# First row tile by halves, norm chunks one pair later, a fourth matmul group further behind, and a last row in narrower column groups

## The chip, the cores and the metric

The kernel runs on one core of a Trainium2 chip. The metric is the device time of one execution in microseconds (us). A profiled execution also has a span, which is 1.7 to 1.9 us shorter than its device time.

## The reference

The reference is the output of a block and its vector-Jacobian product, ten arrays in all. Cut to what matters here:

```python
xn  = layernorm(q)                       # 2048 rows x 1024
out = q + A(xn, k, v, ...) + B(xn, W_gate, W_up, W_down)
# A: shift convolution, long convolution by FFT, times xn
# B: h = relu(xn @ W_gate) * (xn @ W_up);  h @ W_down        (1024 -> 3584 -> 1024)
outputs = out and d(out).grad_out for q, k, v, shift_k, ssm_k, ssm_D, W_gate, W_up, W_down
```

## The kernel before

TensorE is shared by two branches. The branch of B norms the rows, goes through seven blocks of 512 hidden columns (gate, up and gradient matmuls for each row tile of 128), then makes the weight gradients, the output and the gradient of the input. The branch of A does its Fourier transforms as matmuls in between. Four places are touched.

The norm works in chunks of row tiles, (1, 1, 1, 1, 2, 2, 2, 2, 2, 2). It is a generator; each chunk takes three steps:

```python
V.tensor_scalar(out=b(2), in0=b(1), scalar1=LN_EPS, scalar2=None, op0=ALU.add)
V.tensor_copy(out=f(3), in_=b(2))                                     # cast before the root
self.ln_act = nc.scalar.activation(out=f(4), in_=f(3), func=ACT.Sqrt)
yield
root = V.reciprocal(out=f(6), in_=f(4))
...
V.tensor_copy(out=f(10), in_=b(3))                                    # cast after it
self.ln_dve = V.reciprocal(out=self.rstd[:, st0:st0 + n], in_=f(10))
for j in range(n):
    V.tensor_scalar(out=xt[:, j, :], in0=xt[:, j, :], scalar1=self.rstd[:, st:st + 1], ...)   # whole row
    nc.gpsimd.dma_start(out=xn_d[...], in_=xt[:, j, :])               # normalised rows to HBM
```

`flip_xn` transposes a normalised row tile on TensorE and copies it out of PSUM. The first column block (`ahead`) takes the rows two tiles at a time; after each pair one more chunk of the norm is put in, which only matters for later:

```python
yield from grad(sp)
...
if ahead and sp + 4 < HS:
    yield from gate_up(sp + 4)
    chunk()
if n == 1 and sp < 4:
    chunk()
if ahead and sp == 4:
    ... tables()             # Sin tables for branch A
```

PSUM is the memory that the matmuls write their sums to; an eviction is the instruction that takes a finished group out of it and so frees its buffer. `four` makes four PSUM groups of the weight gradients at once. In its first half the fourth group goes one step behind the other three:

```python
for st in range(h + 1):
    for i in range(3 if st < h else 0):
        mm(i, st)
    if st > 0:
        mm(3, st - 1)
```

`grad_x`, the last stage, makes the input's gradient of a row tile in two column groups of 512, each with two reductions on VectorE, then two sums over both, then two last multiplies on ScalarE and two adds.

Branch A starts by loading the normalised rows that the norm has stored, into a tile named xt. The load is issued on the same queue (SyncE's) as all the weights:

```python
def load_xn(self, st):
    xt = st["xt"] = self.xp.tile([P, 16, P], BF16, name="xt")
    self.load_time(xt, self.xn_d, st["cg"])
```

## Time and profile before

| what | value |
|---|---|
| median time at the start (3 runs) | 1929.28 us, from 1925.44 to 1932.4 |
| span of the profiled execution | 1928.7 us |
| TensorE's largest wait, for an eviction near 45 us | 3.4 us |
| its waits for normalised rows, 9 to 30 us | 2.4 us in four |
| its wait in the fourth group of a weight gradient, at 893 us | 0.8 us |
| from its last matmul to the end of the span | 7.96 us |

TensorE is busy for 99% of the span, so only these gaps can be won. A timeline line reads: start, duration, engine, source line, operation, output and input tiles with shapes, how many instructions are merged, and in brackets the idle time before and what ended it. The prediction below shows the lines of the waits, of the start and of the tail.

VectorE's order while the row tiles 4 and 5 (counted from 0, here and below) are normed, and the transposes that wait for it:

```profile
23.54 0.17 DVE L764 CAST ln_s<-ln_b 128x2 f32<-128x2 bf16 x1
...
23.74 0.88 DVE L766 TENSOR_SCALAR ln_x<-ln_x,ln_s 128x1024 bf16<-128x1024 bf16 x2
...
24.54 0.68 DVE L906 SCALAR_TENSOR_TENSOR ru<-ru,ps_u 128x512 bf16<-128x512 bf16 x1
...
29.67 1.07 PE L835 MATMUL pst_x<-ident,ln_x 128*128 128x128 bf16 x16 [0.76 <-DVE ln_x L787]
```

The chunk's subtraction of the mean (L766) comes ahead of an eviction of PSUM (L906). The fourth group's wait, with the matmuls in it:

```profile
893.06 1.24 PE L1063 MATMUL ps_d<-g_nat,hs 128*128 128x512 bf16 x5 [0.84 <-ACT wo L1115]
```

### The profile page before, as it was taken

The page shows a single profiled execution, that of the slowest core. Times are in us where ns is not written, and L with a number is a line of the kernel's source. Part 1 is how long each engine was busy: PE and PEld are TensorE (multiplying, and loading weights), DVE is VectorE, ACT ScalarE, POOL GpSimd, SP SyncE. Part 2 cuts the span into 40 slices and gives each one's busy share as a digit, 9 for nine tenths or more (in the row PEclk, how much of TensorE's full clock was granted, in tenths as well). Part 3 has the DMA queues.
Part 4 walks back from the last instruction along what each step waited for, and adds up shares of the span by engine and source line. Part 5 has one row for each costly group of instructions (what it writes and reads, how often), then busy time and mean ns, then how long its engine had stood idle before and what let it go on. Part 6 is the DMA issues. An engine that isn't in the chain of part 4 may idle for free.

```text
span 1928.7 us, 36213 instructions
## 1 busy us (share of the span) xinstructions
PE 1909.5 (99%) x15526; PEld 881.6 (46%) x15526; DVE 910.5 (47%) x1378; ACT 633.8 (33%) x866; POOL 15.3 (1%) x38
## 2 busy tenths in 40 slices
PE   8999999999999999999999999999999999999998
PEld 3444444444444444444444444444444444444443
DVE  6767767767777754443534444400122222222222
ACT  5754354364354354354354344311000000000000
POOL 1000000000000000000000000000000000000000
PEclk9999999999999999999999999999999999999999
DMA  9975788974874982655662733384999854554451
GB/s 247 265 183 138 181 180 182 222 183 134 185 189 134 249 228 78 173 129 174 164 173 78 173 95 122 104 257 160 239 245 266 200 135 120 120 120 118 118 122 35
DMA packets 616017, 319.08 MB, mean 165 GB/s; under 512 B 450984, under 2 KB 585136, under 8 KB 615856
## 3 DMA queue, kind: packets, MB, share of 16 engines
q1 hardware_dynamic: 605360, 295.79, 62.9%
q10 hardware_dynamic: 9216, 16.78, 2.9%
q0 software_dynamic: 1280, 4.20, 0.6%
q8 instruction: 121, 1.98, 0.4%
q14 instruction: 40, 0.33, 0.1%
HBM read 141.56 MB, written 95.44 MB: 123 GB/s over the span
## 4 chain that ended last, share of the span: by engine, by line
PE 96%; issue 1%; DMA 1%; DVE 1%; ACT 1%; DVEq 0%; SPq 0%; ACTq 0%
PE ps_w L1050 20%; PE ps_x L1232 19%; PE ps_o L1198 10%; PE ps_h L806 10%; PE ps_u L806 10%; PE ps_g L806 10%; PE ps_d L1050 9%; PE ps L72 7%; PE ps_d L1063 1%; PE ps_w L1063 1%; ACT ln_j L743 0%; PE pst L308 0%; DMA ln_x<-in_A_q_dram 0%; DMA wu<-in_B_W_up_dram 0%; DMA wg<-in_B_W_gate_dram 0%
## 5 line engine op out<-in xcount | busy, mean ns | idle before, releaser
L1050 PE MATMUL ps_w<-ugs,xn_nat 128*128 128x512 bf16 x1728 | 383.7, 379 | 0.0
L806 PEld LDWEIGHTS <-xnT 128*128 128x128 bf16 x1792 | 170.5, 98 | 210.4 <-issue 10.6
L1050 PEld LDWEIGHTS <-xn_nat 128*128 128x128 bf16 x1728 | 165.0, 98 | 199.3 <-issue 5.5
L806 PE MATMUL ps_h<-wdT,goT 128*128 128x512 bf16 x896 | 207.7, 382 | 3.4 <-DVE ru L906 3.4
L806 PE MATMUL ps_u<-wu,xnT 128*128 128x512 bf16 x896 | 206.7, 379 | 1.7 <-DMA wu<-in_B_W_up_dram 1.7
L1251 ACT ACTIVATE w<-xn,m 128x512 f32<-128x512 bf16 x32 | 24.3, 807 | 559.0 <-issue 317.2
L806 PE MATMUL ps_g<-wg,xnT 128*128 128x512 bf16 x896 | 206.8, 379 | 1.1 <-DVE xnT L838 0.8
L1232 PE MATMUL ps_x<-wgT,ggT 128*128 128x512 bf16 x896 | 198.6, 379 | 0.0
L1232 PE MATMUL ps_x<-wuT,guT 128*128 128x512 bf16 x896 | 198.6, 379 | 0.0
L1198 PE MATMUL ps_o<-wd,hT 128*128 128x512 bf16 x896 | 193.6, 379 | 0.0
L1050 PE MATMUL ps_d<-g_nat,hs 128*128 128x512 bf16 x768 | 171.9, 379 | 0.0
L1232 PEld LDWEIGHTS <-ggT 128*128 128x128 bf16 x896 | 87.7, 98 | 105.7
L1198 PEld LDWEIGHTS <-hT 128*128 128x128 bf16 x896 | 87.7, 98 | 105.7
L1232 PEld LDWEIGHTS <-guT 128*128 128x128 bf16 x896 | 87.7, 98 | 105.7
L806 PEld LDWEIGHTS <-goT 128*128 128x128 bf16 x896 | 85.6, 98 | 107.0 <-issue 8.1
L319 DVE STREAM_TRANSPOSE flp<-C 128x1024 f32<-128x1024 f32 x48 | 90.5, 1931 | 83.3 <-ACT C L76 83.3
L906 DVE SCALAR_TENSOR_TENSOR ru<-ru,ps_u 128x512 bf16<-128x512 bf16 x112 | 76.5, 683 | 110.3 <-issue 48.6
L967 ACT CAST gh<-ps_h 128x512 bf16<-128x512 f32 x112 | 65.3, 584 | 162.0 <-PE ps_h L806 151.0
L1234 DVE CUSTOM_DVE_ANT_0 gx<-ps_x,gy 128x512 f32<-128x512 f32 x32 | 22.1, 691 | 198.1 <-PE ps_x L1232 198.1
L1148 ACT CAST wi<-ps_w 128x512 bf16<-128x512 f32 x108 | 63.7, 590 | 157.4 <-PE ps_w L1050 152.7
L76 ACT CAST C<-ps 128x1024 bf16<-128x1024 f32 x96 | 92.5, 1015 | 67.1 <-PE ps L72 66.1
L319 DVE STREAM_TRANSPOSE flp<-B 128x1024 f32<-128x1024 f32 x48 | 90.9, 1939 | 47.8 <-ACT B L76 47.8
(172 smaller groups left out, 1519.4 us busy)
## 6 DMA issues: line engine op xcount, KB each, us to landing
ug_d<-ru SPq DMA_DIRECT2D x112, 256.0 KB, 3.6
ugs<-ug_d SPq DMA_DIRECT2D x112, 256.0 KB, 5.2
wg<-in_B_W_gate_dram SPq DMA_DIRECT2D x56, 256.0 KB, 4.3
wu<-in_B_W_up_dram SPq DMA_DIRECT2D x56, 256.0 KB, 3.8
h_d<-ht SPq DMA_DIRECT2D x112, 128.0 KB, 2.1
hs<-h_d SPq DMA_DIRECT2D x56, 256.0 KB, 5.4
out_dram<-wi SPq DMA_DIRECT2D x56, 256.0 KB, 4.0
gt<-in_grad_out_dram SPq DMA_DIRECT2D x32, 256.0 KB, 3.9
```

Of the source, the lines that this page charges most:

```text
L72: self.pri.pin(self.nc.tensor.matmul(out, lhsT=lhsT, rhs=rhs, start=start, stop=stop))
L76: self.pri.pin(self.nc.scalar.copy(out=out, in_=in_))
L319: self.pri.pin(self.nc.vector.transpose(out=df[:, c0:c0 + 32, :], in_=sf[:, c0:c0 + 32, :]))
L806: self.pri.pin(self.nc.tensor.matmul(ps[:], lhsT=xT[:, kt * P:(kt + 1) * P], rhs=w(kt), start=(kt == 0), stop=(kt == self.DT - 1)), always ...
L906: self.pri.pin(nc.vector.scalar_tensor_tensor(out=ru[s][:, 1, :], in0=ru[s][:, 0, :], scalar=0.0, in1=ps[:], op0=ALU.is_gt, op1=ALU.mult))
L967: self.pri.pin(nc.scalar.copy(out=gh[:], in_=ps[:]))
L1050: self.pri.pin(self.nc.tensor.matmul(ps[:], lhsT=lhsT(st), rhs=rhs(st), start=(st == 0), stop=(st == self.ST - 1)))
L1063: self.pri.pin(self.nc.tensor.matmul(ps[i][:], lhsT=lhsT(i, st), rhs=rhs(i, st), start=(st == 0), stop=(st == self.ST - 1)))
L1148: self.pri.pin(nc.scalar.copy(out=wo[0][:, d, :], in_=ps[:]))
L1198: nc.tensor.matmul(ps[:], lhsT=hT[:, kt, :], rhs=self.wd[:, kt, oc], start=(kt == 0), stop=(kt == self.FT - 1))
L1232: nc.tensor.matmul(ps[:], lhsT=T[:, kt, :], rhs=W[:, kt, oc], start=(i == 0), stop=(i == n - 1))
L1251: nc.scalar.activation(out=w[:, oc], in_=xn[:, oc], func=ACT.Identity, scale=m[:, 5:6], bias=m[:, 4:5])
```

## The change

The intent has four parts: start the first matmul earlier by norming and transposing the first row tile in halves, and drop two casts of every chunk; move two norm chunks one pair of row tiles on, so that VectorE does not stand on a late load; let the fourth group lag by three steps, so that its PSUM buffer is free when it is needed; and cut the last row tile into column groups of 512, 256 and 256, so that less work follows the last matmul. The core of the diff:

```diff
-            V.tensor_copy(out=f(3), in_=b(2))
-            self.ln_act = nc.scalar.activation(out=f(4), in_=f(3), func=ACT.Sqrt)
+            self.ln_act = nc.scalar.activation(out=f(4), in_=b(2), func=ACT.Sqrt)
 ...
-            V.tensor_copy(out=f(10), in_=b(3))
-            self.ln_dve = V.reciprocal(out=self.rstd[:, st0:st0 + n], in_=f(10))
+            self.ln_dve = V.reciprocal(out=self.rstd[:, st0:st0 + n], in_=b(3))
 ...
+                for c in (0, 512) if st == 0 else (0,):
+                    xc = xt[:, j, c:c + (512 if st == 0 else D)]
+                    V.tensor_scalar(out=xc, in0=xc, scalar1=self.rstd[:, st:st + 1], ...)
 ...   # flip_xn: transposes and copy in two halves for st == 0
                 if ahead and sp + 4 < HS:
                     yield from gate_up(sp + 4)
+                if ahead and sp in (2, 4):
                     chunk()
 ...   # four
-        for st in range(h + 1):
+        lag = 3
+        for st in range(h + lag):
             for i in range(3 if st < h else 0):
                 mm(i, st)
-            if st > 0:
-                mm(3, st - 1)
+            if st >= lag:
+                mm(3, st - lag)
 ...   # grad_x
-            for ob in range(2):
-                oc = slice(ob * 512, ob * 512 + 512)
+            cuts = (0, 512, 768, D) if last else (0, 512, D)
+            for ob in range(len(cuts) - 1):
+                oc = slice(cuts[ob], cuts[ob + 1])
 ...   # sums added up group by group, the scaled add right behind each group
```

More of the change, by code (lines that the diff above doesn't have):

```diff
@@ L779, in layer_norm @@
                 self.tc.keep_in_program_order(root)
-            V.scalar_tensor_tensor(out=f(5), in0=f(3), scalar=0.5, in1=f(6), op0=ALU.mult, op1=ALU.mult)
+            V.scalar_tensor_tensor(out=f(5), in0=b(2), scalar=0.5, in1=f(6), op0=ALU.mult, op1=ALU.mult)
             V.scalar_tensor_tensor(out=b(3), in0=f(4), scalar=0.5, in1=f(5), op0=ALU.mult, op1=ALU.add)
-            V.tensor_copy(out=f(10), in_=b(3))
-            self.ln_dve = V.reciprocal(out=self.rstd[:, st0:st0 + n], in_=f(10))
+            self.ln_dve = V.reciprocal(out=self.rstd[:, st0:st0 + n], in_=b(3))
             self.pri.now()
@@ L786, in layer_norm @@
                 st = st0 + j
-                V.tensor_scalar(out=xt[:, j, :], in0=xt[:, j, :], scalar1=self.rstd[:, st:st + 1], scalar2=None,
-                                op0=ALU.mult)
+                for c in (0, 512) if st == 0 else (0,):
+                    xc = xt[:, j, c:c + (512 if st == 0 else D)]
+                    V.tensor_scalar(out=xc, in0=xc, scalar1=self.rstd[:, st:st + 1], scalar2=None, op0=ALU.mult)
                 nc.gpsimd.dma_start(out=xn_d[st * P:(st + 1) * P, :], in_=xt[:, j, :])
@@ L832, in flip_xn @@
     def flip_xn(self, st):
-        pst = self.ps.tile([P, self.DT, P], BF16, name="pst_x", tag="bps")
-        for kt in range(self.DT):
-            self.pri.pin(self.nc.tensor.transpose(pst[:, kt, :], self.xn[st][:, kt * P:(kt + 1) * P], self.ident[:]),
-                         always=True)
         xT = self.act_tile("xnT", st)
-        copied = self.nc.vector.tensor_copy(out=xT[:], in_=pst[:].rearrange("p a b -> p (a b)"))
-        if st < 4:
-            self.tc.keep_in_program_order(copied)
+        h = self.DT // 2 if st == 0 else self.DT
+        for k0 in range(0, self.DT, h):
+            pst = self.ps.tile([P, self.DT, P], BF16, name="pst_x", tag="bps")
+            for kt in range(k0, k0 + h):
+                self.pri.pin(self.nc.tensor.transpose(pst[:, kt, :], self.xn[st][:, kt * P:(kt + 1) * P],
+                                                      self.ident[:]), always=True)
+            copied = self.nc.vector.tensor_copy(out=xT[:, k0 * P:(k0 + h) * P],
+                                                in_=pst[:, k0:k0 + h, :].rearrange("p a b -> p (a b)"))
+            if st < 4:
+                self.tc.keep_in_program_order(copied)
         return xT
@@ L1064, in mm @@
                                                stop=(st == self.ST - 1)))
-        for st in range(h + 1):
+        lag = 3
+        done = 0
+        for st in range(h + lag):
             for i in range(3 if st < h else 0):
                 mm(i, st)
-            if st > 0:
-                mm(3, st - 1)
-            if st % 2 == 0 and st:
+            if st >= lag:
+                mm(3, st - lag)
+            if st % 2 and st > lag:
                 yield 1730
                 self.tick()
-                freed(st - 2)
-                freed(st - 1)
+                while done <= st - lag:
+                    freed(done)
+                    done += 1
+        while done < h:
+            freed(done)
+            done += 1
         for i in range(4):
@@ L1224, in grad_x @@
             w = p_ev.tile([P, D], F32, name="w")
-            m = p_sm.tile([P, 8], F32, name="m")
-            for ob in range(2):
-                oc = slice(ob * 512, ob * 512 + 512)
-                ps = self.ps_tile("ps_x")
+            m = p_sm.tile([P, 10], F32, name="m")
+            sums = m[:, 0:6].rearrange("p (a b) -> p a b", b=3)
+            hd = tc.keep_in_program_order
+            last = st == self.ST - 1
+            cuts = (0, 512, 768, D) if last else (0, 512, D)
+            for ob in range(len(cuts) - 1):
+                oc = slice(cuts[ob], cuts[ob + 1])
+                ps = self.ps_tile("ps_x")[:, 0:cuts[ob + 1] - cuts[ob]]
                 i, n = 0, 2 * self.FT
@@ L1231, in grad_x @@
                     for kt in range(self.FT):
-                        nc.tensor.matmul(ps[:], lhsT=T[:, kt, :], rhs=W[:, kt, oc], start=(i == 0), stop=(i == n - 1))
+                        nc.tensor.matmul(ps, lhsT=T[:, kt, :], rhs=W[:, kt, oc], start=(i == 0), stop=(i == n - 1))
                         i += 1
-                V.tensor_tensor_reduce(out=gx[:, oc], in0=ps[:], in1=gy[:, oc], scale=1.0, scalar=0.0, op0=ALU.add,
+                V.tensor_tensor_reduce(out=gx[:, oc], in0=ps, in1=gy[:, oc], scale=1.0, scalar=0.0, op0=ALU.add,
@@ L1235, in grad_x @@
                                        op1=ALU.add, accum_out=m[:, ob:ob + 1])
                 V.tensor_tensor_reduce(out=pr[:, oc], in0=gx[:, oc], in1=xn[:, oc], scale=1.0, scalar=0.0,
-                                       op0=ALU.mult, op1=ALU.add, accum_out=m[:, 2 + ob:3 + ob])
-                if ob == 0:
-                    self.tc.keep_in_program_order(V.scalar_tensor_tensor(
-                        out=gx[:, oc], in0=gx[:, oc], scalar=self.rstd[:, st:st + 1], in1=gt[:, oc], op0=ALU.mult,
-                        op1=ALU.add))
@@ L1242, in grad_x @@
-            hd = self.tc.keep_in_program_order
-            hd(V.tensor_tensor(out=m[:, 4:6], in0=m[:, 0:4].rearrange("p (a b) -> p a b", b=2)[:, :, 0],
-                               in1=m[:, 0:4].rearrange("p (a b) -> p a b", b=2)[:, :, 1], op=ALU.add))
-            hd(V.tensor_scalar(out=m[:, 6:8], in0=m[:, 4:6], scalar1=-1.0 / D, scalar2=None, op0=ALU.mult))
-            hd(V.tensor_scalar(out=m[:, 4:6], in0=m[:, 6:8], scalar1=self.rstd[:, st:st + 1], scalar2=None,
-                               op0=ALU.mult))
+                                       op0=ALU.mult, op1=ALU.add, accum_out=m[:, 3 + ob:4 + ob])
@@ new lines, in grad_x @@
+                if ob:
+                    hd(V.tensor_tensor(out=m[:, 6:8], in0=m[:, 6:8] if ob > 1 else sums[:, :, 0], in1=sums[:, :, ob],
+                                       op=ALU.add))
+                if ob + 2 == len(cuts):
+                    hd(V.tensor_scalar(out=m[:, 8:10], in0=m[:, 6:8], scalar1=-1.0 / D, scalar2=None, op0=ALU.mult))
+                    hd(V.tensor_scalar(out=m[:, 6:8], in0=m[:, 8:10], scalar1=self.rstd[:, st:st + 1], scalar2=None,
+                                       op0=ALU.mult))
@@ L1248, in grad_x @@
+                hd(V.scalar_tensor_tensor(out=gx[:, oc], in0=gx[:, oc], scalar=self.rstd[:, st:st + 1],
+                                          in1=gt[:, oc], op0=ALU.mult, op1=ALU.add))
             o1 = p_ev.tile([P, D], BF16, name="o1")
@@ L1250, in grad_x @@
                 oc = slice(ob * 512, ob * 512 + 512)
-                nc.scalar.activation(out=w[:, oc], in_=xn[:, oc], func=ACT.Identity, scale=m[:, 5:6], bias=m[:, 4:5])
-                if ob:
-                    hd(V.scalar_tensor_tensor(out=gx[:, oc], in0=gx[:, oc], scalar=self.rstd[:, st:st + 1],
-                                              in1=gt[:, oc], op0=ALU.mult, op1=ALU.add))
+                nc.scalar.activation(out=w[:, oc], in_=xn[:, oc], func=ACT.Identity, scale=m[:, 7:8], bias=m[:, 6:7])
                 V.tensor_tensor(out=o1[:, oc], in0=gx[:, oc], in1=w[:, oc], op=ALU.add)
```

## The prediction

> **What bounds the kernel now.** I read the page's busy shares first, then TensorE's own list of waits, then the timeline in order of time around the start, around each of TensorE's waits, and at the end, and last the issue and landing times of the transfers up to 125 us.
>
> The busy table of the page, with busy us, share and instruction count per engine:
>
> ```profile
> PE 1909.5 (99%) x15526; PEld 881.6 (46%) x15526; DVE 910.5 (47%) x1378; ACT 633.8 (33%) x866; POOL 15.3 (1%) x38
> ```
>
> TensorE is idle for only 1928.7 - 1909.5 = 19.2 us, so a change that leaves the matmuls alone can win at most about 1%. The list of TensorE's waits (total us, times, longest) says where that is:
>
> ```profile
> PE ps_h L806 <- DVE ru L906: 3.4, 1, 3.4
> PE pst_x L835 <- DVE ln_x L787: 2.4, 4, 0.8
> PE ps_u L806 <- DMA wu<-in_B_W_up_dram: 1.7, 1, 1.7
> PE ps_d L1063 <- ACT wo L1115: 0.8, 1, 0.8
> PE ps_g L806 <- DVE xnT L838: 0.8, 1, 0.8
> ```
>
> Beyond these lie the 1.48 us before the first warming matmul and 8 us after the last one (the end of the matmuls at 1920.74 against a span of 1928.7). All parts of the change aim at these waits, except that for the weights (1.7 us).
>
> Timeline of the first normalised row tile (start, us, engine, line, idle before):
>
> ```profile
> 6.90 0.19 ACT L743 ACTIVATION_READ_ACCUMULATOR ln_j<-ln_x 128x1 f32 x1
> 7.00 0.19 ACT L775 ACTIVATE ln_s<-ln_s 128x1 f32<-128x1 f32 x1
> ...
> 8.09 0.15 DVE L782 CAST ln_s<-ln_b 128x1 f32<-128x1 bf16 x1
> ...
> 8.28 0.16 DVE L783 RECIPROCAL rstd<-ln_s 128x1 f32<-128x1 f32 x1
> 8.48 0.49 DVE L787 TENSOR_SCALAR ln_x<-ln_x,rstd 128x1024 bf16<-128x1024 bf16 x1
> ...
> 9.71 0.68 DVE L838 COPY xnT<-pst_x 128x1024 bf16<-128x1024 bf16 x1
> ```
>
> The square root (L775) starts when ScalarE finishes the row sum of the second tile, not when its input is cast. After it comes a serial chain: cast, reciprocal, whole-row multiply, eight transposes (9.02), whole-row copy, and the first useful matmul at 10.45.
>
> Timeline around the large wait:
>
> ```profile
> 36.29 0.41 SPq L723 DMA_DIRECT2D ln_x<-in_A_q_dram  x1
> ...
> 41.26 1.06 ACT L743 ACTIVATE ln_j<-ln_x 128x1024 bf16<-128x1024 bf16 x1 [4.66 <-DMA ln_x<-in_A_q_dram]
> ...
> 43.48 0.17 DVE L757 TENSOR_SCALAR ln_b<-ln_s 128x2 bf16<-128x2 f32 x1 [4.54 <-ACT ln_j L743]
> ...
> 44.69 0.68 DVE L906 SCALAR_TENSOR_TENSOR ru<-ru,ps_u 128x512 bf16<-128x512 bf16 x1
> ...
> 45.41 3.56 PE L806 MATMUL ps_h<-wdT,goT 128*128 128x512 bf16 x8 [3.38 <-DVE ru L906]
> ```
>
> A row chunk of the norm (rows 8 and 9, needed only much later) was put ahead of the eviction L906 on VectorE. Its load lands at 41.17, so VectorE stands 4.54 us on it, the PSUM buffer stays full, and TensorE stops 3.38 us. The next eight matmuls then take 3.56 us in place of the usual 1.89.
>
> **What the Trainium skill says.** "TensorE: Matmul & The Clock Gate", Part 1: the array falls to half rate after an idle window of about 3.4 us and needs such a window of work to return. The trace agrees: 3.38 us idle, the eight matmuls after it about 430 ns apart against 216 ns elsewhere, mean granted clock 0.83 from 40 to 50 us and 1.00 in the stretches beside it. The same page, specifications, calls ScalarE and VectorE strict FIFO: that is the eviction behind the chunk above. Its section on 56 ns against 53.3 ns gives about 2.5 ns fixed per matmul; the last row's 28 matmuls from 1908.48 to 1914.53 are 216.1 ns apart, which is 512/2.4 GHz + 2.8 ns. "VectorE: DVE Perf Modes", errata section, gives (N+151)/0.96 ns for a one-element-per-cycle operation: 691 ns at N = 512, and the reduction L1234 takes 0.69 us here.
>
> **The change, part by part.**
>
> *Start.* (a) The cast before the root buys the first tile nothing, for ScalarE is busy until 7.0. The cast after it is on the path: 8.28 - 8.09 = 0.19 us. (b) Halves: the multiply costs 0.16 us at one element and 0.49 at 1024, so about 0.33 at 512, and the second half ends about 0.6 after the start. Before, from the multiply's start to the first gate matmul were 10.45 - 8.48 = 1.97 us. Now: half multiply 0.33 + wait 0.05 + four transposes about 0.37 (0.62 for eight, of which the pipeline is fixed) + 0.07 + half copy about 0.42 (0.68 minus 256 cycles of 0.96 GHz at two elements a cycle) + 0.06 = 1.30. Gain 0.67. Only four of the matmuls (0.86 us) run before the second half is needed, and that half is about 0.4 us behind, so it doesn't show. Together 0.85 us. The up weights land at 10.35, 11.10, 11.85 and 12.56; the up matmuls moved from 12.63 to about 11.75 take them at steps of 0.43 us and just miss waiting. (c) Whether the 0.85 reaches the end depends on the later transposes, which wait for their tile at 17.29 (0.17), 21.38 (0.79) and 29.67 (0.76 us). Chunk two gains from earlier VectorE work and one cast, so it comes about as much earlier as TensorE does. In chunks three and four the casts (two of 0.2 us; the one in chunk three stands behind an eviction of 0.68 us and may save more) take about 0.4 each off the 0.79 and 0.76. Sum for the start: 0.85 - 0.1 + 0.4 + 0.4 = about 1.55, say 1.5 us.
>
> *Row chunks one pair on.* The wait of 3.38 goes, and the slow clock with it: 3.56 - 1.89 = 1.67. Sum 5.05 us. The chunk moves to where the next one stood (row sum at 53.21), which made TensorE wait for nothing; the next goes behind the two gradient matmul groups at 55.73 and pushes the Sin tables (60.6 to 75 us) back by some 5 us. They are first needed at 102.29 (RH), so there is room. But TensorE, 6.5 us earlier, comes closer to its transfers: the second column block's gate weights land at 56.80 to 59.05 and were wanted at 62.64; now they are wanted at about 56.1, 56.5, 57.0, 57.4. They move up by about 1.5 us, as two 256 KB stores of the moved chunk no longer lie before them (landings there are 0.75 us per 256 KB). Also the gate eviction at 52.48 writes a buffer freed by a store that landed at 50.45, and now wants it at 45.7; with four PSUM buffers TensorE feels that about 5 us later, so hardly. I take off 0.7 us: 4.35.
>
> *Fourth group three steps behind.* The first matmul into the fourth PSUM buffer comes after 9 matmuls instead of 3, 6 x 0.216 = 1.3 us later. The only wait there, 0.84 us at 893.06, goes; the first and third use of this helper show no wait. The deferred loads come under 2 us later and are used 10 us later. One yield fewer per use lets the other branch lag by 1.76 us of pace; TensorE works on without it from 1271 to 1340 us, so that costs nothing. Gain 0.8 us.
>
> *Last row in 512, 256, 256.* After the last matmul the two reductions shrink from 691 to 424 ns (estimate from the formula above): 2 x 0.267 = 0.53. The scaled add L1253 (step 1925.25 - 1924.41 = 0.84) leaves the chain, for it now runs while ScalarE makes the first w (0.80); the last add then waits for the second w: 1922.95 + 1.52 = 1924.47 instead of starting at 1925.25, so this part gives 0.75. The tail, with the lines of before:
>
> ```profile
> 1920.77 0.69 DVE L1234 CUSTOM_DVE_ANT_0 gx<-ps_x,gy 128x512 f32<-128x512 f32 x1 [9.87 <-PE ps_x L1232]
> ...
> 1922.95 1.52 ACT L1251 ACTIVATE w<-xn,m 128x512 f32<-128x512 bf16 x2 [22.66 <-issue]
> 1923.80 0.69 DVE L1255 TENSOR_TENSOR o<-gx,w 128x512 bf16<-128x512 f32 x1 [0.93 <-ACT w L1251]
> 1924.41 0.74 DVE L1253 SCALAR_TENSOR_TENSOR gx<-gx,rstd,gt 128x512 f32<-128x512 f32 x1
> 1925.25 0.69 DVE L1255 TENSOR_TENSOR o<-gx,w 128x512 bf16<-128x512 f32 x1
> ```
>
> Against it stand 56 more matmuls at about 2.5 ns (0.14). Gain 0.53 + 0.75 - 0.14 = 1.1 us. The final store stays at 1928.7 - 1925.94 = 2.8 us.
>
> Sum: 1.5 + 4.35 + 0.8 + 1.1 = 7.75 us, 0.4%. From the measured 1929.28: about 1921.5.
>
> **The rivals.** (1) Transfers take the place of the wait: from 50 to 75 us landings follow each other without a gap. If the gate and up weights of block two don't move up, TensorE waits there for 2 to 4 us, and could cool again: gain only 3 to 5 us, 1925. For it: the even spacing of landings. Against: the two stores that leave that stretch, and the slack of 10.8 us before. (2) The moved chunk and the pushed tables make a new wait at 60 to 80 us, where VectorE is busy 9.90 of 10 us (60 to 70): a stop of up to 3 us, with the slow clock 5: about 1926. Against: an eviction there was already 1.9 us late (69.84 against 67.9) and TensorE didn't wait; the load is the same in sum. (3) The start is bound by ScalarE's order: the casts are hidden and the 0.85 us is taken back at 17.29 to 29.67; 0.8 us less gain. (4) A new instruction order puts the root before the next row sum (1 us each time) and wins 1 us more: 1920.
>
> **Range and chances.** The parts alone spread from 3 to 9.5 us of gain; the three runs of before lie within 1925.44 and 1932.4, so a median can be off by 2 or 3 us. Range 1916 to 1927.5. A gain over 2% would take 38.6 us, twice all of TensorE's idle time; a loss over 2% would need a stall that nothing here suggests. Faster 0.005, same 0.985, slower 0.01.
>
> **What would show it.** Right: no wait of the gradient matmuls for L906 near 40 us, granted clock 1.00 from 40 to 50, the first gate matmul near 9.6, no wait for wo at 890, and about 6.8 us from the last matmul to the end of the span. Wrong: new waits for wg or wu at 55 to 61 us, a wait for a PSUM eviction at 60 to 80 us, or waits for ln_x as long as before with the first matmul earlier.

## The result, and the profile after

| | before | after |
|---|---|---|
| median time, first comparison (4 runs each) | 1928.61 us | 1925.75 us |
| lowest and highest | 1925.44, 1932.4 | 1924.11, 1926.66 |
| span of the profiled execution | 1928.7 us | 1922.2 us |

The ratio is 0.9983, with a 95% interval of 0.9964 to 1.0003: the same within 2%. A ratio here is the mean time of one kernel's fast runs over that of the other's fast runs in the same rounds, so it is not quite the ratio of the medians. Two repetitions of the changed kernel, told below, gave 0.9971 and 0.9975 of five rounds each. The ratios of the three sets, times the medians of before, make a gain of 3.3, 5.6 and 4.8 us. The prediction said 7.75 us. The time lies inside the predicted range, but 2 to 4.5 us of the expected gain are missing.

The page's busy line of the changed kernel:

```profile
PE 1888.9 (98%) x15350; PEld 886.8 (46%) x15582; DVE 909.1 (47%) x1366; ACT 635.0 (33%) x867; POOL 15.8 (1%) x38
```

TensorE seems to have lost 20 us of busy time, but it has 15350 matmul records against 15582 weight loads: 232 records are missing from this trace. Its busy time cannot be set against that of before. The starts of weight loads, which are complete, are the landmarks used below.

TensorE's waits, in the form of the prediction's list (us in total, times, longest):

```profile
PE pst_x L837 <- DVE ln_x L787: 2.0, 3, 1.4
...
PE ps_g L805 <- DMA wg<-in_B_W_gate_dram: 1.3, 3, 0.7
```

The wait for the eviction and that for wo are gone. The wait for normalised rows has not shrunk as expected, with one of 1.4 us in it. A wait for gate weights, wg, is new. The start, from the timeline:

```profile
8.26 0.62 DVE L787 TENSOR_SCALAR ln_x<-ln_x,rstd 128x512 bf16<-128x512 bf16 x2
...
8.92 0.61 PE L837 MATMUL pst_x<-ident,ln_x 128*128 128x128 bf16 x8
...
9.49 0.74 DVE L839 COPY xnT<-pst_x 128x512 bf16<-128x512 bf16 x2
...
9.96 1.90 PE L805 MATMUL ps_g<-wg,xnT 128*128 128x512 bf16 x8 [0.43 <-DVE xnT L839]
```

The first gate matmul starts at 9.96 instead of 10.45. VectorE's order at the place that was shown of before:

```profile
23.13 0.68 DVE L908 SCALAR_TENSOR_TENSOR ru<-ru,ps_u 128x512 bf16<-128x512 bf16 x1
...
23.73 0.16 DVE L764 CAST ln_s<-ln_b 128x2 f32<-128x2 bf16 x1
...
24.19 0.88 DVE L766 TENSOR_SCALAR ln_x<-ln_x,ln_s 128x1024 bf16<-128x1024 bf16 x2
...
29.65 1.07 PE L837 MATMUL pst_x<-ident,ln_x 128*128 128x128 bf16 x16 [1.41 <-DVE ln_x L787]
```

Everything before it is earlier, but now the eviction (L908, the former L906) stands ahead of the chunk's cast and subtraction. This order is that of the built program: it is the same in all three traces of the changed kernel, and the old one in both of the kernel before. The subtraction begins at 24.19 instead of 23.74, and the transposes of tiles 4 and 5 begin at 29.65, as before. TensorE alone, from 40 us to the third column block:

```profile
41.85 1.89 PE L805 MATMUL ps_h<-wdT,goT 128*128 128x512 bf16 x7
...
57.39 3.62 PE L805 MATMUL ps_g<-wg,xnT 128*128 128x512 bf16 x16
...
103.51 0.60 PE L805 MATMUL ps_g<-wg,xnT 128*128 128x512 bf16 x2 [0.70 <-DMA wg<-in_B_W_gate_dram]
```

The gradient matmuls at 41.85 wait for nothing, where they stood 3.38 us before. The third block's first gate matmuls at 103.51 wait for a load. And the tail:

```profile
1915.60 0.42 DVE L1247 CUSTOM_DVE_ANT_0 gx<-ps_x,gy 128x256 f32<-128x256 f32 x1 [4.62 <-PE ps_x L1245]
...
1917.07 0.47 DVE L1258 SCALAR_TENSOR_TENSOR gx<-gx,rstd,gt 128x256 f32<-128x256 f32 x1
1917.25 1.52 ACT L1263 ACTIVATE w<-xn,m 128x512 f32<-128x512 bf16 x2 [22.27 <-issue]
1918.09 1.40 DVE L1264 TENSOR_TENSOR o<-gx,w 128x512 bf16<-128x512 f32 x2 [0.55 <-ACT w L1263]
```

The reduction works on 256 columns in 0.42 us, the scaled add (L1258) runs beside the first half of w, and the two last adds follow each other.

Landmarks of all three traces of the changed kernel against both of before show where the gain lies (start of the first weight load of each stage, us; the second and third columns are each kernel's mean):

| stage | before (2) | after (3) | gain so far | gain in the stage |
|---|---|---|---|---|
| second column block | 61.50 | 57.44 | 4.1 | 4.1 |
| third column block | 106.86 | 103.87 | 3.0 | -1.1 |
| W_down's gradient | 681.92 | 678.95 | 3.0 | 0.0 |
| gate and up weights' gradient | 906.74 | 902.62 | 4.1 | 1.2 |
| input's gradient | 1533.36 | 1529.28 | 4.1 | 0.0 |
| end of the span | 1928.5 | 1923.2 | 5.3 | 1.2 |

The fourth group and the last row bring 2.4 us, slightly more than the predicted 1.9. Start and row chunks together bring 3.0 instead of 5.85, and lose 1.1 us of what they had between the second and the third block.

### The profile page after: what moved, and what is told of

Its sections match the earlier page's. It is cut to its first block, busy times and chain, and to the rows that moved or that the text cites. A ratio compares the mean times of both kernels' runs of the same rounds, so it can differ in the third digit from the quotient of the medians.

```text
span 1922.2 us, 36073 instructions
## 1 busy us (share of the span) xinstructions
PE 1888.9 (98%) x15350; PEld 886.8 (46%) x15582; DVE 909.1 (47%) x1366; ACT 635.0 (33%) x867; POOL 15.8 (1%) x38
## 4 chain that ended last, share of the span: by engine, by line
PE 92%; issue 3%; ACT 2%; DVE 2%; DMA 1%; SPq 1%; ACTq 0%; DVEq 0%
PE ps_w L1053 19%; PE ps_x L1245 19%; PE ps_o L1207 10%; PE ps_h L805 9%; PE ps_u L805 9%; PE ps_g L805 9%; PE ps_d L1053 9%; PE ps L72 7%; PE ps_d L1066 1%; ACT ln_j L743 1%; PE pst L308 0%; PE ps_w L1066 0%; SPq L816 0%; DMA wu<-in_B_W_up_dram 0%; DMA ugs<-ug_d 0%
## 5 line engine op out<-in xcount | busy, mean ns | idle before, releaser
L1053 PE MATMUL ps_w<-ugs,xn_nat 128*128 128x512 bf16 x1672 | 375.9, 379 | 5.8 <-issue 4.3
L805 PE MATMUL ps_h<-wdT,goT 128*128 128x512 bf16 x863 | 202.4, 379 | 2.9 <-issue 1.8
L1245 PE MATMUL ps_x<-wgT,ggT 128*128 128x512 bf16 (+1 forms) x907 | 197.8, 372 | 0.9
L1245 PE MATMUL ps_x<-wuT,guT 128*128 128x512 bf16 (+1 forms) x906 | 197.6, 372 | 0.9
L1053 PE MATMUL ps_d<-g_nat,hs 128*128 128x512 bf16 x741 | 167.4, 379 | 3.2 <-issue 2.7
L908 DVE SCALAR_TENSOR_TENSOR ru<-ru,ps_u 128x512 bf16<-128x512 bf16 x112 | 76.5, 683 | 108.4 <-issue 43.0
L1053 PEld LDWEIGHTS <-hs 128*128 128x128 bf16 x768 | 72.7, 98 | 88.9 <-issue 4.2
```

The costliest lines, as they stand in the source:

```text
L805: self.pri.pin(self.nc.tensor.matmul(ps[:], lhsT=xT[:, kt * P:(kt + 1) * P], rhs=w(kt), start=(kt == 0), stop=(kt == self.DT - 1)), always ...
L908: self.pri.pin(nc.vector.scalar_tensor_tensor(out=ru[s][:, 1, :], in0=ru[s][:, 0, :], scalar=0.0, in1=ps[:], op0=ALU.is_gt, op1=ALU.mult))
L1053: self.pri.pin(self.nc.tensor.matmul(ps[:], lhsT=lhsT(st), rhs=rhs(st), start=(st == 0), stop=(st == self.ST - 1)))
L1245: nc.tensor.matmul(ps, lhsT=T[:, kt, :], rhs=W[:, kt, oc], start=(i == 0), stop=(i == n - 1))
```

## The experiments

Twelve runs were made, with five rounds each, on three different chips, so times are compared as ratios; the places in the traces are compared across them.

### The kernel before, again (r_before)

Edit: none.

> The kernel before once more, as a control for the noise and for what in its first trace belongs to that one execution. Theory A: the 1.7 us wait for the up weights at 258 us in the first trace was a hiccup of that execution, not of the kernel, so here it is gone or stands elsewhere, and the gain of 6.5 us between the two first traces was flattered by it. Rival B: the wait belongs to the kernel before and is back within 0.3 us of 1.7. Both expect the 3.4 us wait of the gradient matmuls for the eviction near 42 us again, and the ratio to the kernel before within 0.2% of 1.

Measured: 1929.34 us, 0.9997 [0.9984, 1.0009], span 1928.3. Its waits on TensorE:

```profile
PE ps_h L806 <- DVE ru L906: 3.0, 1, 3.0
...
PE ps_g L806 <- DMA wg<-in_B_W_gate_dram: 1.2, 2, 1.0
```

The large wait was 2.98 us here and 3.38 us in the first trace. Here the clock stayed up; two traces alone do not show whether the length of the wait or the moment on which it fell decided this. Stretches of five us of both executions (length, busy us of PE, PEld, DVE, ACT and POOL, then the granted clock, DMA share and GB/s), first of the first trace:

```profile
45.00:50.00 5.00, 4.58 (x14) 1.80 (x14) 3.93 (x14) 2.91 (x7) 0.00 (x0) 0.66 1.07 163
```

and of the repetition:

```profile
45.00:50.00 5.00, 4.75 (x22) 1.97 (x22) 3.96 (x15) 2.85 (x7) 0.08 (x1) 1.00 0.72 196
```

The repetition had a full clock, and reached the second block at 60.57 instead of 62.42. Yet both reach the third block at the same time, 106.89 and 106.82: the repetition waits 1.0 us there for wg, which the first trace does not. In these two executions the slow clock cost nothing at the third block. The wait of 1.7 us for up weights at 258 us was 0.9 us here, so neither theory held as it stood; what this wait does is told under the row chunks in the part on the prediction.

### The kernel after, again (r_after)

Edit: none to the changed kernel.

> The changed kernel once more. Theory A: true gain 4.0 to 5.5 us (ratio 0.9972 to 0.9979), made of about 3 us that are left of the row chunks' move after 110 us, 0.8 of the fourth group, 1.2 of the tail, and nothing of the start. Rival B: gain of 6 us or more (ratio under 0.9969), as the first traces differ by 6.5. In the trace: transposes of row tiles 4 and 5 at 29.6 to 29.7 us again, waits for the gate weights of 1 to 1.5 us near 103 us again.

Measured: 1924.55 us, 0.9971 [0.9958, 0.9983], span 1922.8. The first gate matmul started at 10.37 this time, 0.4 us later than in the first trace of after, and yet the transposes of tile 2 started at 17.02, against 17.01. The first matmul's time does not reach tile 2. The wait for wg at the third block was 1.7 us, and the block started at 103.67.

### The row chunks alone (x_chunks)

```diff
 # kernel before
                     yield from gate_up(sp + 4)
+                if ahead and sp in (2, 4):
                     chunk()
```

> The kernel before with only the two row chunks moved one pair on. Theory A: the 3.4 us wait and the slow clock go (second column block's first gate matmul at about 57.4 us instead of 62.6), but by 137 us only about 3 us of it are left, because the last row chunks of the norm come only 3 us earlier and the transfer queue stands behind their store. Total gain about 3 us (ratio 0.9984). Rival B: the losses at 80 to 106 us come from the other parts of the change; then the whole 5 us stay (ratio 0.9974).

Measured: 1927.69 us, 0.9991 [0.9978, 1.0003], span 1924.9. The wait near 45 us is gone, the second block starts at 57.03 (61.5 in the mean of before), the third at 104.92 (106.86): of 4.5 us, 1.9 are left at the third block. W_down's gradient starts at 678.52, 3.4 us earlier than before: this trace has no wait for up weights near 258 us, where the two of before have 1.7 and 0.9 us. The timed gain of 1.7 us is less than the trace's 3.6, but the profiled execution was the fastest of its five, and the interval reaches from a gain of 4.2 to a loss of 0.6 us.

### The start alone (x_start)

```diff
 # kernel before, with layer_norm and flip_xn of after
-            V.tensor_copy(out=f(3), in_=b(2))
-            V.tensor_copy(out=f(10), in_=b(3))
 ...   # and the halves of the first tile
```

> The kernel before with only the start changed (first tile by halves, casts gone). Theory A: first gate matmul 0.4 to 0.7 us earlier, but the transposes of row tiles 4 and 5 at 29.6 to 29.7 us as before, since the evictions of the up groups now stand ahead of that chunk's subtraction on VectorE: gain 0 us (ratio 0.9995 to 1.0005). Rival B: 0.7 to 1.5 us earlier there, and the changed kernel lost it only in company with the moved chunks.

Measured: 1930.34 us, 0.9999 [0.9986, 1.0013], span 1928.5. The first gate matmul starts at 9.99 and the transposes of tile 3 at 20.60, 0.7 us earlier than the mean of before. The transposes of tiles 4 and 5 start at 29.53, as in the repetition of before, and are waited for 1.4 us. Nothing is won from there on. The large wait even grew to 4.83 us, as the chunk's load landed later. So the start alone is worth nothing that can be measured.

### The fourth group and the last row alone (x_ends)

```diff
 # kernel before, with four and grad_x of after
+        lag = 3
 ...
+            cuts = (0, 512, 768, D) if last else (0, 512, D)
```

> The kernel before with only the two late parts: fourth group three steps behind, and the last row in 512, 256, 256. Theory A: they add up undisturbed: from the first weight-gradient matmul (near 682 us) to the first input-gradient one (near 906 us) 1.1 us less than the 224.8 us of before, and from the end of the matmuls to the end of the span 1.2 to 1.3 us less; together about 2.3 us (ratio 0.9988). Rival B: what the fourth group doesn't wait for is waited for by the transfers of the normalised rows behind it, so that only the tail's 1.2 us are left (0.9994). The 3.4 us wait near 42 us stays under both.

Measured: 1928.65 us, 0.9994 [0.9981, 1.0007], span 1926.2. The time is 1 us lower, but the interval holds 1. The trace is clear on the two stages. In place of the five matmuls that waited 0.84 us, 21 go in one run:

```profile
889.68 4.70 PE L1063 MATMUL ps_d<-g_nat,hs 128*128 128x512 bf16 x21
```

From W_down's gradient to that of gate and up it is 223.66 us here, and 223.67 to 223.69 in the three executions of after, against 224.70 to 224.87 in the four without this part: 1.1 us. From the last matmul to the end of the span it is 1.3 us less in the changed kernel (6.64 against 7.96).

The row chunk's wait was 3.98 us in this run, for the same code as in before. After it the clock fell again: from the start of the waiting matmuls to that of the next up matmuls it is 6.87 us, 6.87 in the first trace of before, 6.86 in x_start, and 5.18 where nothing waits (after). The drop costs 1.68 to 1.69 us after waits of 3.38, 3.98 and 4.83 us alike. The traces say why: the granted clock is 0.50 for 3.41 us in each of the three (45.46 to 48.87 us in the first trace of before, 47.37 to 50.78 in x_start, 47.94 to 51.35 here), and half of that is 1.7 us.

### Chunk ahead of the eviction (a_less)

Here the eviction near 23 us is told to go behind the chunk's subtraction, as it stood before the change.

```diff
 # kernel after
+                    self.ln_less = less            # the subtraction of the chunk of tiles 4 and 5
 ...
+                with self.tc.issue_after(self.ln_less.ins) if ahead and s == 2 else ExitStack():
                     self.pri.pin(nc.vector.scalar_tensor_tensor(out=ru[s][:, 1, :], ...))
```

> The changed kernel with one ordering edge more: the eviction of the third up group goes behind the subtraction of row tiles 4 and 5 on VectorE. Theory A: the start's gain was lost to this order alone; the transposes of tiles 4 and 5 come 0.6 to 0.8 us earlier (about 28.9 us in place of 29.65), and the second column block at about 56.5 instead of 57.2. Whether it reaches the end depends on the weights of the third column block; 0 to 0.7 us. Rival B: another link of that chain (the up eviction ahead of the reciprocal, or the load) holds the transposes at 29.5 or later.

Measured: 1924.96 us, 0.9974 [0.9961, 0.9986], span 1920.4.

```profile
23.63 0.88 DVE L766 TENSOR_SCALAR ln_x<-ln_x,ln_s 128x1024 bf16<-128x1024 bf16 x2
...
24.42 0.68 DVE L911 SCALAR_TENSOR_TENSOR ru<-ru,ps_u 128x512 bf16<-128x512 bf16 x1
...
29.13 1.07 PE L839 MATMUL pst_x<-ident,ln_x 128*128 128x128 bf16 x16 [0.72 <-DVE ln_x L789]
```

With the old order the transposes start at 29.13 instead of 29.65, and wait 0.72 instead of 1.41 us. So VectorE's order is what swallowed the start's gain at this place. The second block starts at 56.66, 0.5 us earlier than in the first trace of after. The time is not lower: the changed kernel's own ratios were 0.9971 and 0.9975. They were run at other times. The third block again starts with the landing of wg, 101.79 and 101.83.

### The first load of branch A on another queue (a_xtq)

The load of xt waits for the last normalised rows' store, and wg stands behind it on SyncE's queue. Of the changed kernel:

```profile
95.39 1.96 SPq L88 DMA_DIRECT2D xt<-xn_d  x2
...
99.52 2.27 SPq L798 DMA_DIRECT2D wg<-in_B_W_gate_dram  x4
```

The last store of normalised rows landed at 95.25, and xt was issued at 95.39. The experiment issues the first xt from GpSimd.

```diff
 # kernel after
+        if st["gi"] == 0:
+            self.pri.now()
+            for u in range(2):
+                self.nc.gpsimd.dma_start(out=xt[64 * u:64 * u + 64], in_=self.tview(self.xn_d, st["cg"])[u])
+        else:
             self.load_time(xt, self.xn_d, st["cg"])
```

> The changed kernel with the first two loads of the normalised rows for the other branch on GpSimd's queue. Theory A: the third column block's gate weights come late only because they stand behind these loads in SyncE's queue, which wait for the last row chunk's store; now they are issued 3 to 5 us earlier and TensorE doesn't wait for them: third block at 102.2 instead of 103.5 to 103.7, gain 1.3 us there. Rival B: the transfers themselves are saturated there; the weights land no more than 0.5 us earlier and the gain is under 0.5 us.

Measured: 1924.99 us, 0.9975 [0.9961, 0.9989], span 1923.7. The first piece of wg is issued at 96.20 and lands at 101.05, 2.4 us earlier than in the first trace of after. But the two halves of xt land at 102.08 and 105.15, and the third and fourth pieces of wg at 105.69 and 106.41, later than the third and fourth in after (105.22 and 105.98). The third block starts at 103.15, no real gain, although its first piece had been there for 2.1 us: TensorE itself came late, as the second block started at 57.58 and two waits of 0.5 and 0.4 us for ScalarE lay between; and it then waited 1.0 us for the third piece. The queue's order alone was not the limit. The Trainium skill, "DMA: Bandwidth & Descriptors", section on rules for kernel authors, says that spreading transfers over several issuing engines gains no bandwidth, as they all run on the same 16 DMA engines; the landing times of this run agree: one piece earlier, two later.

### Half of the Sin tables later (a_split)

ScalarE is busy 9.58 and 9.97 us of the ten from 70 to 80 and from 80 to 90 us in the changed kernel, 7.18 and 9.41 in the kernel before: the Sin tables and the norm's last chunks now share this time. Four loads of function tables of 1.28 us each lie between 78 and 92 us. The experiment puts the second half of the tables behind the last chunk.

```diff
 # kernel after
+        yield                       # in tables(), ahead of its second half
+        pri.late()
 ...
-                        tables()
+                        tabs = tables()
+                        next(tabs)
 ...
+                if n == 1 and sp == 2:
+                    ... next(tabs, None)      # behind the last chunk
```

> The changed kernel with the second half of the tables (inverse transforms) built after the last row chunk, so that ScalarE loads its Sin and Sqrt tables twice less (2 x 1.28 us) in the stretch from 70 to 95 us, where it is 96 to 99% busy. Theory A: ScalarE's saturation there is what takes back the row chunks' gain: the waits for the gradient evictions (0.5 us) go, the last row chunk is stored about 3 us earlier, the third column block starts 1 to 2 us earlier. Rival B: the saturation delays only work that has slack: third block unchanged within 0.4 us.

Measured: 1924.54 us, 0.9968 [0.9956, 0.9981], span 1923.4. The last chunk's store landed at 93.89, against 95.25, 93.87 and 95.86 in the three executions of after, so it may be earlier by a little and may not. The third block started at 103.30, with wg landing at 103.26, and TensorE waited 1.1 us for hT of branch A (0.2 us in the three executions of after) and 1.4 us for up weights near 254 us (0.1, 0.8 and 1.5 us there in the three). ScalarE was relieved from 80 to 90 us (7.41 us busy in place of 9.97), not from 70 to 80 (9.71). No gain over the changed kernel can be seen.

### The load of branch A without its dependence (a_xfree)

This kernel is wrong: the first xt is read from another input, the incoming gradient, with the same shape, so that it need not wait for the normalised rows. Five outputs have relative errors of 0.30 to 0.36.

```diff
 # kernel after
-        self.load_time(xt, self.xn_d, st["cg"])
+        self.load_time(xt, self.xn_d if st["gi"] else self.g, st["cg"])
```

> Wrong results on purpose (the first channel group's loads take the upstream gradient in place of the normalised rows): the changed kernel, same order of instructions, but the transfer that stands ahead of the third column block's gate weights no longer waits for the last row chunk. Theory A: that wait takes back what the moved row chunks gained: the gate weights' transfers are issued at about 96 us or before and land before 102, TensorE doesn't wait for them, third block at 101.6 to 102.3 instead of 103.5 to 103.7, gain 1.3 to 2 us there. Rival B: SyncE's queue stands as long behind the gradient stores, or the transfers are saturated: third block within 0.4 us of the changed kernel's.

Measured: 1921.88 us, 0.9962 [0.995, 0.9975], span 1920.7, against 1923.82 us of the changed kernel in the same rounds (r_after2). All five runs (1920.8 to 1922.53) lie below all five of r_after2 (1922.88 to 1926.52).

```profile
89.88 1.37 SPq L88 DMA_DIRECT2D xt<-in_grad_out_dram  x2
...
95.43 2.83 SPq L798 DMA_DIRECT2D wg<-in_B_W_gate_dram  x4
```

xt is issued 5.5 us and wg 4.1 us earlier than in the lines above, the first piece of wg lands at 100.09, the third block starts at 102.33 and W_down's gradient at 676.11, 2.8 us earlier than the mean of after. So the dependence of wg on the norm's last store, through xt and the queue's order, costs the changed kernel about 2 us. (The edit frees xt itself too, but TensorE's list of waits has none for xt in the changed kernel.)

### Chunks closer together (a_c67)

```diff
 # a_less, with the two chunks moved
+                if ahead and sp == 2:
+                    chunk()
                     yield from gate_up(sp + 4)
-                if ahead and sp in (2, 4):
+                if ahead and sp == 2:
                     chunk()
```

> The changed kernel with the ordering edge of tiles 4 and 5, and the two row chunks placed otherwise: one just before the last gate and up pair of the first block, one just after it, so that both lie some 5 us earlier than in the change. Theory A: the last row chunk is then stored 1 to 3 us earlier and the third block starts at 100.5 to 101.5; but the second chunk's load lands at about 53 us, and evictions behind it stop TensorE for up to 1 us near 55. Rival B: that stop is 2 us or more (the wait of before in a new place), and nothing is won on the change.

Measured: 1925.02 us, 0.9981 [0.9968, 0.9993], span 1924.6. The last chunk's store came later, not earlier (98.31), wg landed at 106.72, and the third block started at 106.76: the largest wait for wg of all runs, 2.8 us. The stop near 55 us that both theories had did not come. The attempt failed, and it shows from the other side that a later store gives a later third block.

### The order and the split tables together (a_both)

Edit: those of a_less and a_split.

> The changed kernel with both the ordering edge and the split tables. If the two gains of 0.7 us (second block) and of the earlier last row chunk add up, the third block starts at 101.5 to 102.5 and the time is 1 to 2 us under the changed kernel's of the same rounds; if the third block is bound by its transfers, no difference over 0.5 us.

Measured: 1922.9 us, 0.9969 [0.9956, 0.9981], span 1921.0. This is 0.9 us below r_after2 in the same rounds, with intervals that overlap for the most part. The third block started at 103.20, not at the hoped 101.5 to 102.5. It does not beat the changed kernel clearly.

### The kernel after, a third time (r_after2)

Edit: none to the changed kernel.

> The changed kernel a third time, beside the variants: ratio 0.9970 to 0.9984, third block at 103.5 to 103.7 us, transposes of tiles 4 and 5 at 29.6 to 29.7 us.

Measured: 1923.82 us, 0.9975 [0.9962, 0.9989], span 1924.7. The profiled execution was the slowest of its five. The third block started at 104.44, with wg landing at 104.40.

## Why the prediction was right or wrong

**The total.** The range and the class held; the gain was 3.3 to 5.6 us by time and 5.3 us by traces, not 7.75. By spans against the two traces of before, the parts alone gave 0 (start), 3.6 (chunks) and 2.3 (ends); their sum of 5.9 agrees with 5.3 for the whole. By time they gave 0.2, 1.7 and 1.2 us, each with some 2.5 us to either side, which is too coarse to settle a part.

**The fourth group** was right: predicted 0.8, measured 1.1 us. The wait is gone; of the other 0.3 us nothing was tested. The prediction's counts are off, its difference is not: by the code the first matmul of the fourth group comes after 12 of the others instead of 6, not after 9 instead of 3.

**The last row** was right: predicted 1.1, measured 1.2 us in the landmarks' means. The steps held too: the reductions took 0.42 us as estimated, and the narrow matmuls stand (1906.23 - 1903.17)/28 = 0.1093 us apart, so that they cost the predicted 0.14 us.

**The start** was wrong: predicted 1.5, measured 0. The step that failed is (c), which lets the 0.85 us pass to the end and adds 0.4 us each from chunks three and four. The first gate matmul came 0.0 to 0.4 us earlier in the three executions of after than in the mean of the two of before, not 0.85: in the first trace the transposes start at 8.92, right behind the warming matmuls, and not at 8.64, the estimated half multiply and 0.05 us after 8.26. Step (b) left these 24 matmuls out. They start about 427 ns apart at first and 216 ns apart later, and the change came at 4.4 and 5.6 us in the two traces of before, at 6.1, 7.3 and 6.9 in the three of after; it differs between executions of one kernel, so part of what the halves could win was lost by chance. And the gains that followed (0.2 us at tile 2, 0.6 us at tile 3 in the means) ended at 29.65. There the rebuilt program has another order on VectorE, in x_start as in after: an eviction and the product after it stand ahead of the chunk of tiles 4 and 5. a_less put the order back and got 0.5 us at this place. Why the build chose this order is not shown. Rival (3) foresaw that the gain would be taken back by 29.67, but put it down to ScalarE's order; it was VectorE's.

**The row chunks** were right in their mechanism and wrong in their size: predicted 4.35, measured 3.0 together with the start. The wait is gone and the clock stays at 1.00. The second block starts 5.2 us earlier between the two first traces, 4.1 us in the means, as one execution of before had no slow clock. What failed is "I take off 0.7 us": with the start at nothing, 5.05 less 3.0, that is 2.05 us, had to come off. The loss is rival (1) in kind, transfers that take the place of the wait, but at the third block, where the prediction did not look, and not at the second. The rule behind it can be read from the landmarks. The third block starts at the later of two times: 44.4 us after the second block's start, which is what TensorE needed where its loads were there in time (44.40 in before, 44.39 in x_start), and the landing of the first piece of wg.

| execution | second block + 44.4 | wg lands | third block starts |
|---|---|---|---|
| before | 106.82 | 106.77 | 106.82 |
| r_before | 104.97 | 106.84 | 106.89 |
| x_start | 108.68 | 106.89 | 108.67 |
| x_chunks | 101.43 | 104.88 | 104.92 |
| after | 101.58 | 103.47 | 103.51 |
| r_after | 101.60 | 103.63 | 103.67 |
| r_after2 | 102.35 | 104.40 | 104.44 |
| a_less | 101.06 | 101.79 | 101.83 |
| a_c67 | 101.85 | 106.72 | 106.76 |

x_ends and a_split follow it as closely; a_xtq, a_xfree and a_both start 0.6 to 1.2 us after both times, with small waits for ScalarE in between. In before the two times meet, so every us that TensorE wins shows only as far as wg moves too. Against the mean of before, wg moved by 2.4 to 3.3 us, as the last store of normalised rows moved by 2.8 us (97.83 to 94.99 in the means). a_xfree cut this dependence and won about 2 us.

The 1.67 us that the prediction counted for the slow clock were a right measure (1.68 to 1.69 in three executions) but not a sure gain: with and without the drop, the two executions of before start their third block within 0.07 us of each other. After the longer waits of x_start and x_ends the slow clock does reach the third block, which starts 1.8 and 1.6 us later there than in the mean of before. But it goes no further than a second meeting point. The fourth piece of the up weights used near 258 us lands between 257.56 and 258.40 in all four traces with the old chunk places. TensorE waits for it 1.7 and 0.9 us in the two of before and about 0.1 us or less in the two late ones, and W_down's gradient starts at 681.66 to 682.17 in all four, although the second block started between 60.57 and 64.28. This is read from the traces; no run moved that load alone. The prediction's window of about 3.4 us was not contradicted: 2.98 us of waiting left the clock alone.

**What stays open.** Why the last store moved by 2.8 us and not by the 4.1 us that TensorE had won by then is argued, not shown: ScalarE is nearly full from 70 to 90 us, but a_split relieved half of that time without a clear effect. From the store's landing to that of wg it took 7.9 us in a_less and 9.8 in r_after, for the same store time; what the transfers in between did differently was not followed up.

**What the prediction said would show it.** No wait for L906, a clock of 1.00 from 40 to 50 us, and no wait for wo: all came true. The tail was 6.64 us and not "about 6.8". The first gate matmul "near 9.6" failed (9.96 to 10.37), and its mark for a wrong start came, waits for ln_x as long as before with the first matmul earlier: 2.0 us in the first trace of after, 1.8 and 2.0 in the repetitions, against 2.4 and 1.7. The waits for wg came at 103, outside the 55 to 61 us that the prediction watched.

## What to carry to other kernels

When a wait is taken away, follow each later stage's first operand back through the queue that loads it to the store or engine that lets it go: the gain is the smaller of TensorE's and that chain's, and here the two were level in the kernel before. Add up a wait and its slow clock only as far as the next such meeting point. A change can make the build choose another order on an engine, so a gain at the first instruction counts only where it is seen again some tiles later.

## What the Trainium skill lacked or had wrong

- "TensorE: Matmul & The Clock Gate", in its terms, puts the penalty of a throttled stretch at its length times (1 - K/N), K/N being the granted share of the clock; that agrees here, with 3.41 us at 0.50 and 1.68 to 1.69 us lost. It lacks that the drop can come after the work has resumed: in x_ends the matmuls went on at 46.90 us, five of them started 210 to 219 ns apart, and the clock fell at 47.94.
- The same page says that the number of slow matmuls at the start differs from execution to execution. It lacks what this does to a kernel that lays warming matmuls ahead of its first work: the same 24 lasted from 6.83 us (before) to 8.31 us (a_less), and the transposes queue behind them in order (8.92 to 9.47 us in the three executions of after), so 0.2 us won in the norm need not show.
- The same page, "Back-to-back issue gap", gives N / 2.4 + 2.5 ns for a single gap and says that a stream of weight loads and matmuls at N = 512 runs at about 131 ns per matmul. Here such streams kept to the formula: 216.1 ns at 512 columns, 109.3 ns at 256 (109.2 by the formula).
- "VectorE: DVE Perf Modes", errata section, states (N+151)/0.96 ns for an fp32 tensor_tensor add at N = 512 and 2048 only. The reduction of the last row, another operation, followed it too: 691 ns at 512 columns, 423 and 425 ns at 256 (424 by the formula).
- "DMA: Bandwidth & Descriptors" has the issuing engine wait on the first DMA's semaphore before it issues a dependent one, but not what follows for a kernel with one loading queue: a load that waits for a late store (xt, issued at 95.39 after a store that landed at 95.25) holds back the weights behind it, about 2 us of the whole here (a_xfree).
